# Second products of an attention and feed-forward kernel as 64-row pairs between key tiles, three visits per batch instead of seven

## The chip, the cores and the metric

The kernel runs on one core of one Trainium2 chip. The metric is device time in microseconds (us) of one execution; before the change it is 431.01, the median of three runs (430.65 to 431.02). Five engines work side by side: TensorE (PE, its weight loads shown as PEld), VectorE (DVE), ScalarE (ACT), GpSimd (POOL) and SyncE (SP). They meet through semaphores. PE writes its results into PSUM, which has eight banks here; DVE and ACT read them out.

## The reference

```
batch, n_heads, seq, head_dim = (8, 12, 448, 64)      # q, k, v: float32
q_n = q / (norm(q) + 1e-06);  k_n = k / (norm(k) + 1e-06)
scores = q_n @ k_n.T / tau                             # tau = 0.1
attn = exp(scores - max);  attn = attn / (sum(attn) + 1e-09)
x = (attn @ v), heads side by side                     # 3584 tokens x 768
h = x @ w_in                                           # 768 -> 2048
out = max(0.01 * h, h) @ w_out                         # 2048 -> 768
```

## The kernel before

**The work.** A *pair* is two heads of one batch (`s`, 48 of them, six per batch). Its q and k are loaded, squared and summed along the head (`squares` on POOL, `sums` on DVE), turned into norms (`roots`, an Ln and an Exp on ACT), divided by them (`normalise` on DVE) and transposed (`transposes`, from pair 12 on by a DMA of SP's queue). `hold` is a one-column copy on POOL that waits for the end of `normalise` ahead of the next `squares`. `roots` is two ACT instructions, so it stands in ACT's order between other activations.

**Key tiles.** A pair has three key tiles of 128 keys; the remaining 64 keys of two pairs share a fourth (`ki == 3`). `key_tiles` (L244) multiplies each key tile into two banks: two products, one per head, each on 64 rows of the array, since a head has 64 dimensions. The shared tile takes four products on quarters of the array. ACT then takes the exponential of both banks at once (L268).

**Attention of two pairs.** `attend(j)` (L527) sums the exponentials of four heads (`totals`, 16 products on 32-column strips into one bank, then an Ln and an Exp on ACT, L290 and L291), multiplies them with v (`products`, 32 strips into two banks), and `scale` writes the result to `xT` (DVE, L310).

**Feed-forward.** A *chunk* `c` is 384 columns of tokens (even `c`) or 512 (odd `c`), which become complete when batch `c` is attended. `first(c, m)` (L324) makes one of 16 slices of the hidden layer: six products of 128 rows into one bank and a Prelu on ACT (L340). `second(c, ts, half)` (L359) makes half of the output columns of 128 tokens: 16 products of 128 rows by 384 columns into one bank (L363), and a copy on DVE (L374). After the second half the rows are stored by SP's queue.

**The order of the work.** The order on each engine is that in which the program issues it. In the loop over batches (L599) the first and second groups of the chunk before stand in `queue`. From batch 2 on a batch has seven visits (`whole`, L582). Each issues, where it has one, the attention of two pairs (three of the seven do), then three key tiles, then the normalisation of one later pair (`sums`, `roots`, `normalise`, `transposes`, loads, `hold`, `squares` of the pair behind it, L612 to L631), then as many groups of `queue` as a share worked out from their costs allows (L604, L634). One group of the queue stays for the next batch. Behind the loop the last attention is followed by the group that is left and by the whole chunk 7.

**Banks.** `banks` (L77) deals the eight banks while the program is built: the one, or the aligned two, that was dealt longest ago, with those left out that are kept under a name until `given_back`. Whoever writes a bank waits for whoever read it last.

Of the kernel before, what the change touches and what calls it, by code (L numbers as in the profile page):

```python
# [8 lines left out]
F32 = mybir.dt.float32  # L9
# [7 lines left out]
def kernel(  # L17
# [10 lines left out]
    nc = tc.nc  # L28
    B, H, S, D = q.shape
    N_tok, D_model = out.shape  # L30
# [6 lines left out]
    NPAIR = H // 2  # L37
    NSLOT = B * NPAIR
    NQ = NPAIR // 2
    KT = D_model // 128  # L40
    MT = D_ff // 128
    HALF = D_model // 2
# [2 lines left out]
    ATTEND = 5500  # L45
    BLOCK = 1800
    SOON = 2
    assert REM == 64 and D == 64

    ctx.enter_context(tc.manual_schedule())  # L50
# [26 lines left out]
    def banks(count, keep=None, which=None):  # L77
        lo, hi = (0, 8) if not deals["apart"] else (0, 4) if count == 2 else (4, 8)
        x = which if which is not None else min(
            (i for i in range(lo, hi, count) if not set(range(i, i + count)) & set(kept.values())),  # L80
            key=lambda i: max(age[i : i + count]),
        )
        deals["n"] += 1
        age[x : x + count] = [deals["n"]] * count
        if keep:
            kept[keep] = x
        return ps[:, x] if count == 1 else ps[:, x : x + count]

    def given_back(keep):
        deals["n"] += 1  # L90
        age[kept.pop(keep)] = deals["n"]

# [26 lines left out]
    def load_qk(s, engs=(nc.sync, nc.sync)):  # L119
        if s >= NSLOT:  # L120
            return
        b, h0 = s // NPAIR, 2 * (s % NPAIR)
        q_h = ldp.tile([128, 2, 4, D], F32, name="q_h")
        k_h = ldp.tile([128, 2, 3, D], F32, name="k_h")
        engs[0].dma_start(out=q_h[:, :, 0:3], in_=main(q, b, h0, 2))
        engs[1].dma_start(out=k_h, in_=main(k, b, h0, 2))
        for i, (x, eng) in enumerate(zip((q, k), engs)):
            eng.dma_start(  # L128
                out=q_h[64 * i : 64 * i + 64, :, 3],
                in_=x[b, h0 : h0 + 2, MAIN:S].rearrange("h p d -> p h d"),  # L130
            )
        raw[s] = (q_h, k_h)
# [35 lines left out]
    def sums(s, parts=(0, 1)):  # L168
        if s >= NSLOT:
            return  # L170
        if s not in ss:
            ss[s] = smp.tile([128, 14], F32, name="ss")
        for i in parts:
            o = ss[s][:, 0:8] if i == 0 else ss[s][:, 8:14]
            nc.vector.tensor_reduce(  # L175
                o.rearrange("p (h t) -> p h t", h=2), sqs[s][i], axis=AX.X, op=ALU.add
            )

    def roots(s):
        if s >= NSLOT:  # L180
            return
        nc.scalar.activation(ss[s], ss[s], func=AF.Ln, bias=tiny)
        nc.scalar.activation(ss[s], ss[s], func=AF.Exp, scale=0.5)  # L183
        if s < 2:
            nc.scalar.activation(ss[s], ss[s], func=AF.Identity, bias=eps)
# [3 lines left out]
    def normalise(s):  # L189
        if s >= NSLOT:  # L190
            return
        r = smp.tile([128, 14], F32, name="r")
        if s >= 2:
            nc.vector.tensor_scalar_add(ss[s], ss[s], 1e-6)  # L194
        nc.vector.reciprocal(r, ss[s])  # L195
        qn[s] = qnp.tile([128, 7, 2, D], BF16, name="qn")
        for x, lo, hi, r0 in ((raw[s][0], 0, 4, 0), (raw[s][1], 4, 7, 8)):
            nt = hi - lo
            nc.vector.tensor_tensor(  # L199
                qn[s][:, lo:hi],  # L200
                x.rearrange("p h t d -> p t h d"),
                r[:, r0 : r0 + 2 * nt].rearrange("p (h t) -> p t h", h=2)
                .unsqueeze(3).to_broadcast([128, nt, 2, D]),
                op=ALU.mult,
            )
# [19 lines left out]
    def transposes(s):  # L225
        if s >= NSLOT:
            return
        dst = qtp.tile([128, 7, 128], BF16, name="qkT")
        qkT[s] = dst.rearrange("p t c -> p (t c)")
        if s >= DMA_FROM:  # L230
            nc.sync.dma_start(
                out=dst, in_=qn[s].rearrange("p t h d -> p (t h d)"), transpose=True
            )
            return
        tp = transposed()
        one(tp, s, 0, 7)
        nc.vector.tensor_copy(out=dst, in_=tp)  # L237
# [81 lines left out]
    def chunk_cols(c):  # L319
        return (0, MAIN) if c % 2 == 0 else (MAIN, 512)  # L320
# [27 lines left out]
    def rows_of(c, x, end):  # L348

        bb, rest = divmod(x, S)  # L350
        r0 = (2 * (c // 2) + bb) * S
        if rest >= MAIN:
            cnt = min(S - rest, end - x)
            return out[r0 + rest : r0 + rest + cnt], cnt
        t, p0 = divmod(rest, 128)
        cnt = min(128 - p0, end - x)
        return out[r0 : r0 + MAIN].rearrange("(p t) n -> t p n", t=3)[t, p0 : p0 + cnt], cnt

    def second(c, ts, half):  # L359
        c0, n = chunk_cols(c)  # L360
        po2 = banks(1)
        for m in range(MT):
            nc.tensor.matmul(  # L363
                out=po2[:, :HALF],
                lhsT=hT[c][:, m, ts * 128 : (ts + 1) * 128],
                rhs=w_out_sb[:, m, half * HALF : (half + 1) * HALF],
                start=(m == 0), stop=(m == MT - 1),
            )
        if half == 0:
            osb[c, ts] = osp.tile([128, D_model], F32, name="osb")  # L370
        o = osb[c, ts]
        last = c == B - 1 and ts == n // 128 - 1
        cut = HALF // 2 if last and half == 1 else HALF
        nc.vector.tensor_copy(out=o[:, half * HALF : half * HALF + cut], in_=po2[:, :cut])  # L374
        if cut < HALF:
            nc.scalar.copy(out=o[:, half * HALF + cut : (half + 1) * HALF], in_=po2[:, cut:HALF])
        if half == 1 or last:
            h0 = half * HALF if last else 0
            x, end, row = c0 + ts * 128, c0 + (ts + 1) * 128, 0
            while x < end:  # L380
                dst, cnt = rows_of(c, x, end)
                eng = nc.scalar if cut < HALF and row else nc.sync
                eng.dma_start(
                    out=dst[:, h0 : (half + 1) * HALF],
                    in_=o[row : row + cnt, h0 : (half + 1) * HALF],
                )
                x += cnt
                row += cnt


    work = {}
# [49 lines left out]
    def hold(x):  # L441
        seen = smp.tile([128, 1], F32, name="seen")
        gp.tensor_copy(out=seen, in_=x)  # L443
# [83 lines left out]
    def attend(j):  # L527
        totals(j)
        po = banks(2)
        for e in range(2):  # L530
            products(j, e, po[:, e])
        for e in range(2):
            scale(j, e)
# [63 lines left out]
    ]  # L597
    queue = []
    for b in range(1, B):  # L599
        queue += work[b - 1]  # L600
        units = opened if b == 1 else whole
        costs = [BLOCK + (ATTEND if at is not None else 0) for at, _, _ in units[1:] + [(2, 0, 0)]]
        for i, (at, tiles, ahead) in enumerate(units):
            share = (sum(g[0] for g in queue[:-1]) + sum(costs[i:])) / (len(units) - i) - costs[i]  # L604
            if b > 1 and i == 0:
                at = -1
            if at is not None:
                attend(b * NQ + at)
                load_v(b * NQ + at + 2)
            key_tiles([(b * NPAIR + p, ki) for p, ki in tiles])  # L610
            done = 0
            s = b * NPAIR + ahead if ahead else NSLOT  # L612
            if s < NSLOT:
                sums(s)
                roots(s)
            if b == 1 and i < 2:

                if i == 1:
                    cost, fn = queue.pop(0)
                    fn()  # L620
                    done += cost
                transposes(NPAIR + 4 + i)
            if s < NSLOT:
                normalise(s)
                if s >= DMA_FROM:
                    transposes(s)

                for n in (s + 2,) if s <= NPAIR + 6 else (s + 2, s + 3) if s == NPAIR + 7 else (s + 3,):
                    load_qk(n)
                hold(qn[s][:, 6, 0, 0:1])  # L630
                squares(s + 1)  # L631
            if at == 1:
                load_v_rem(b + 1)
            while len(queue) > 1 and (i == len(units) - 1 or done + queue[0][0] / 2 <= share):  # L634
                cost, fn = queue.pop(0)
                fn()
                done += cost
    attend(B * NQ - 1)
    for cost, fn in queue + work[B - 1]:
        fn()  # L640


# [33 lines left out]
```

## Time and profile before

| what | value |
|---|---|
| median of three runs | 431.01 us |
| the profiled execution's own time | 430.29 us |
| its span, first to last instruction | 428.4 us |
| PE busy, products | 414.7 us, 3315 of them |
| ACT busy | 255.4 us |
| DVE busy | 195.9 us |
| POOL busy | 137.3 us |
| second products, L363 | 896, 326 ns each from start to end |
| first products, L333 | 326 ns with 384 columns, 379 ns with 512 |
| strips, L279 | 352 to 356 ns each, four at once |
| exponential of a key tile, L268 | 144, 917 ns each |

A page of the profile describes one execution. Busy time of an engine is a union: products that run at the same time count once, and products overlap, each beginning before the one ahead has ended. So the length of one product is not its price; the price is read from how far apart products begin. The chain that ended last goes back from the last instruction, at each step to what released it or to the instruction before it on its engine. The timeline lists the instructions of all engines by their start; what stands in brackets is the idle time of the engine ahead of one and what ended it. Two batches together last 98.7 us there (batches 2 and 3 from 81.17 to 179.86, batches 4 and 5 from there to 278.54), so the middle of the kernel repeats every two batches.

### The profile page before, as it was taken

How to read it: one execution, taken by the hardware profiler on the slowest of the kernel's cores; microseconds unless marked ns; L12 is line 12 of the kernel's file. 1: busy time of each engine (PE TensorE's matmuls, PEld its weight loads, DVE VectorE, ACT ScalarE, POOL GpSimd, SP SyncE). 2: the span in 40 equal slices, each digit the busy share in tenths (PEclk: the TensorE clock that was granted, in tenths of full speed). 3: DMA queues.
4: the chain of work that ended last, by engine and by line, in shares of the span. 5: the costliest groups of instructions: out<-in, count | busy, mean ns of one | idle time of the engine just before them, and what ended most of it. 6: DMA issues, size and time to landing. Idle time of an engine off the chain costs nothing.

```text
span 428.4 us, 8636 instructions
## 1 busy us (share of the span) xinstructions
PE 414.7 (97%) x3315; PEld 208.2 (49%) x3329; DVE 195.9 (46%) x412; ACT 255.4 (60%) x448; POOL 137.3 (32%) x208
## 2 busy tenths in 40 slices
PE   7689999999999999999999999999999999999995
PEld 3234455544455555544455555544455555554563
DVE  5885867643453545354353554553444541220021
ACT  3987785667644785567553786658635586434300
POOL 4767533534124243513324132621424110000000
PEclk9999999999999999999999999999999999999999
DMA  7999997994558455953658456864448422110022
GB/s 174 187 240 229 211 217 135 186 207 104 108 121 166 103 125 95 224 108 84 127 101 160 104 127 129 168 113 136 91 103 161 100 61 42 39 73 2 0 75 74
DMA packets 102889, 53.66 MB, mean 125 GB/s; under 512 B 68928, under 2 KB 97856, under 8 KB 102848
## 3 DMA queue, kind: packets, MB, share of 16 engines
q1 hardware_dynamic: 77296, 40.98, 38.4%
q0 software_dynamic: 25056, 11.80, 22.0%
q8 instruction: 26, 0.43, 0.4%
q10 hardware_dynamic: 496, 0.33, 0.2%
q14 instruction: 15, 0.12, 0.1%
HBM read 45.61 MB, written 11.01 MB: 132 GB/s over the span
## 4 chain that ended last, share of the span: by engine, by line
PE 91%; DVE 3%; DMA 2%; issue 1%; SPq 1%; ACT 1%; POOL 0%; POOLq 0%; DVEq 0%
PE ps L363 35%; PE ps L333 34%; PE ps L279 13%; PE ps L256 9%; DVE qn L199 2%; DMA q_h<-in_q_dram 1%; PE ps L213 1%; DMA q_h<-in_k_dram 1%; SPq L128 1%; ACT pe L268 0%; DVE xT L310 0%; DVE ss L175 0%; DVE ss L194 0%; DVE r L195 0%; DVE qkT L237 0%
## 5 line engine op out<-in xcount | busy, mean ns | idle before, releaser
L268 ACT ACTIVATE pe<-ps 128x896 bf16<-128x896 f32 x144 | 122.5, 917 | 51.1 <-PE ps L256 50.0
L363 PE MATMUL ps<-w_out_sb,hT 128*128 128x384 bf16 x896 | 151.9, 326 | 0.0
L333 PE MATMUL ps<-xT,w_in_sb 128*128 128x384 bf16 (+1 forms) x757 | 150.6, 352 | 1.0 <-DVE xT L310 0.4
L363 PEld LDWEIGHTS <-hT 128*128 128x128 bf16 x896 | 85.2, 98 | 62.9 <-issue 8.4
L333 PEld LDWEIGHTS <-w_in_sb 128*128 128x128 bf16 x768 | 73.1, 98 | 72.9 <-issue 7.8
L340 ACT ACTIVATE hT<-ps 128x384 bf16<-128x384 f32 (+1 forms) x128 | 65.9, 541 | 46.7 <-PE ps L333 46.6
L374 DVE COPY osb<-ps 128x384 f32<-128x384 f32 (+1 forms) x56 | 30.9, 552 | 98.6 <-PE ps L363 92.1
L443 POOL CAST seen<-qn 128x1 f32<-128x1 bf16 x47 | 8.7, 184 | 207.7 <-DVE qn L199 201.9
L175 DVE TENSOR_REDUCE ss<-sq 128x8 f32<-128x512 f32 (+1 forms) x96 | 56.6, 614 | 19.2 <-POOL sq L164 16.9
L256 PE MATMUL ps<-qkT 64*128 64x448 bf16 (+1 forms) x384 | 46.1, 358 | 3.6 <-ACT pe L268 2.3
L164 POOL TENSOR_TENSOR sq<-q_h 128x512 f32<-128x512 f32 x46 | 47.8, 1038 | 3.7 <-DMA q_h<-in_k_dram 2.9
L310 DVE TENSOR_TENSOR xT<-ps,rb 128x448 bf16<-128x448 f32 x48 | 27.8, 619 | 32.5 <-ACT rb L291 32.5
L194 DVE TENSOR_SCALAR ss<-ss 128x14 f32<-128x14 f32 x46 | 9.2, 199 | 67.5 <-ACT ss L183 67.4
L164 POOL TENSOR_TENSOR sq<-k_h 128x384 f32<-128x384 f32 x46 | 37.8, 822 | 0.0
L290 ACT ACTIVATE rb<-ps 128x448 f32<-128x448 f32 x24 | 13.1, 544 | 38.9 <-PE ps L279 38.9
L279 PE MATMUL ps<-pe,v_b 128*32 128x448 bf16 x576 | 35.6, 353 | 0.0
L199 DVE TENSOR_TENSOR qn<-q_h,r 128x512 bf16<-128x512 f32 x48 | 33.5, 698 | 1.6
L256 PEld LDWEIGHTS <-qkT 64*128 64x128 bf16 (+1 forms) x384 | 13.0, 96 | 37.9 <-issue 31.5
L199 DVE TENSOR_TENSOR qn<-k_h,r 128x384 bf16<-128x384 f32 x48 | 26.5, 551 | 0.0
L268 ACT ACTIVATE pr<-ps 128x896 bf16<-128x896 f32 x24 | 22.2, 925 | 0.2 <-PE ps L256 0.2
L279 PEld LDWEIGHTS <-v_b 128*32 128x32 bf16 x576 | 15.2, 97 | 11.9 <-issue 0.4
L151 POOL DMA_DIRECT2D v_rem<-in_v_dram x32 | 20.4, 645 | 0.1
(40 smaller groups left out, 177.8 us busy)
## 6 DMA issues: line engine op xcount, KB each, us to landing
q_h<-in_q_dram SPq DMA_DIRECT2D x48, 192.0 KB, 3.1
k_h<-in_k_dram SPq DMA_DIRECT2D x47, 192.0 KB, 3.1
out_dram<-osb SPq DMA_DIRECT2D x30, 192.0 KB, 3.5
v_b<-in_v_dram POOLq DMA_DIRECT2D x24, 192.0 KB, 5.1
out_dram<-osb SPq DMA_DIRECT2D x12, 384.0 KB, 3.3
w_in_sb<-in_moe_w_in_dram POOLq DMA_DIRECT2D x4, 768.0 KB, 10.1
w_out_sb<-in_moe_w_out_dram POOLq DMA_DIRECT2D x2, 1536.0 KB, 18.5
q_h<-in_q_dram SPq DMA_DIRECT2D x48, 32.0 KB, 3.5
```

The source lines that it names most:

```text
L151: gp.dma_start(out=vrb[b % 2][lo : lo + 64, :, g], in_=r[g])
L164: eng.tensor_tensor(sq, x, x, op=ALU.mult)
L175: nc.vector.tensor_reduce(o.rearrange("p (h t) -> p h t", h=2), sqs[s][i], axis=AX.X, op=ALU.add)
L199: nc.vector.tensor_tensor(qn[s][:, lo:hi], x.rearrange("p h t d -> p t h d"), r[:, r0 : r0 + 2 * nt].rearrange("p (h t) -> p t h", h=2) .u ...
L256: nc.tensor.matmul(out=out[:, a, :S], lhsT=x[rows, c0:c1], rhs=x[rows, 0:S], start=True, stop=True,)
L268: nc.scalar.activation(out=dst, in_=sc[:, :, :S], func=AF.Exp, scale=inv_tau)
L279: nc.tensor.matmul(out=x[32 * g : 32 * g + 32, :S], lhsT=weights(g, ki) if ki < 3 else rem(g), rhs=pe[s][:, ki, a, :] if ki < 3 else pr[j] ...
L310: nc.vector.tensor_tensor(xT[m][:, 2 * jj + e, half * S : (half + 1) * S], pos.pop((j, e))[:, :S], rbs[j], op=ALU.mult,)
L333: nc.tensor.matmul(out=pm[:, :n], lhsT=w_in_sb[:, kt, m * 128 : (m + 1) * 128], rhs=xT[c // 2][:, kt, c0 : c0 + n], start=(kt == 0), stop= ...
L340: nc.scalar.activation(out=hT[c][:, m, :n], in_=pms.pop((c, m))[:, :n], func=AF.Prelu, alpha=0.01)
L363: nc.tensor.matmul(out=po2[:, :HALF], lhsT=hT[c][:, m, ts * 128 : (ts + 1) * 128], rhs=w_out_sb[:, m, half * HALF : (half + 1) * HALF], st ...
L374: nc.vector.tensor_copy(out=o[:, half * HALF : half * HALF + cut], in_=po2[:, :cut])
```

## The change

Up to batch 2 the loop stays, but batch 2 leaves six groups of the queue instead of one: three of the four token tiles of chunk 1. It also normalises one pair more in its last visit. From batch 3 on a batch has three visits. Each attends two pairs, then issues seven key tiles in three lots of two, three and two. Between the first and the second lot, and between the second and the third, stands one part of a token tile's second products, made by `both_halves`. Behind the key tiles come two normalisations and five or six first groups, the second normalisation in the middle of them. The token tiles are those of the chunk before the last, so they trail a chunk behind. A chunk with four of them puts its last one, by `second`, among the first groups of the first two visits.

`both_halves` takes the 128 rows of each hidden slice as two times 64 rows, which are multiplied at the same time into two banks. Part 0 adds up the upper rows for one half of the output columns and the lower rows for the other; part 1 does the crossed combinations into the same banks, then DVE copies both and the rows are stored. Ahead of the first products of part 1 stand two empty PE instructions that wait for the last products of part 0 in the same bank. The two banks are kept from part 0 to the copies. Behind the loop stand the last attention, six second groups of chunk 6 and the whole chunk 7.

```diff
+    APART = 6
+    MT_APART = 1
...
+    def both_halves(c, ts):
+        state = {}
+        def part(n):
+            if n == 0:
+                state["po"] = banks(2, ("rows", c, ts))
+            po2 = state["po"]
+            last = {}
+            for m in range(MT):
+                for h in range(2):
+                    rows, half = slice(64 * h, 64 * h + 64), h ^ n
+                    if n == 1 and m == 0:
+                        tc.add_manual_dep(
+                            nc.tensor.nop().ins,
+                            state["last"][half].ins.name,
...
+                        )
+                    last[half] = nc.tensor.matmul(
+                        out=po2[:, half, :HALF],
+                        lhsT=hT[c][rows, m, ts * 128 : (ts + 1) * 128],
+                        rhs=w_out_sb[rows, m, half * HALF : (half + 1) * HALF],
+                        start=(n == 0 and m == 0), stop=(n == 1 and m == MT - 1),
+                    )
+            state["last"] = last
+            if n == 1:
+                o = osp.tile([128, D_model], F32, name="osb")
+                for half in range(2):
+                    nc.vector.tensor_copy(
+                        out=o[:, half * HALF : (half + 1) * HALF], in_=po2[:, half, :HALF]
+                    )
+                given_back(("rows", c, ts))
+                store(o, c, chunk_cols(c)[0] + ts * 128, 0, D_model)
+        return lambda: part(0), lambda: part(1)
...
+    def norm(s):
+        if s >= NSLOT:
+            return
+        sums(s)
+        roots(s)
+        normalise(s)
+        transposes(s)
+        load_next(s)
+        hold(qn[s][:, 6, 0, 0:1])
+        squares(s + 1)
...
-    for b in range(1, B):
+    for b in range(1, 3):
         queue += work[b - 1]
+        keep = 1 if b == 1 else APART
...
+    visits = [
+        (-1, [(0, 0), (0, 1)], [(0, 2), (1, 0), (1, 1)], [(1, 2), (1, 3)]),
+        (0, [(2, 0), (2, 1)], [(2, 2), (3, 0), (3, 1)], [(3, 2), (3, 3)]),
+        (1, [(4, 0), (4, 1)], [(4, 2), (5, 0), (5, 1)], [(5, 2), (5, 3)]),
+    ]
+    tiles_left = [(1, ts) for ts in range(MT_APART, 4)]
+    for b in range(3, B):
+        firsts = [fn for _, fn in work[b - 1][:MT]]
+        more = []
+        if len(tiles_left) > len(visits):
+            c, ts = tiles_left.pop()
+            more = [lambda half=half: second(c, ts, half) for half in range(2)]
+        for i, (at, *parts) in enumerate(visits):
+            j, rows = b * NQ + at, both_halves(*tiles_left.pop(0))
+            attend(j)
+            load_v(j + 2)
+            if at == 1:
+                load_v_rem(b + 1)
+            for n, part in enumerate(parts):
+                key_tiles([(b * NPAIR + p, ki) for p, ki in part])
+                if n < 2:
+                    rows[n]()
+            fill_in = [firsts.pop(0) for _ in range(len(firsts) // (len(visits) - i))]
+            if more:
+                fill_in.insert(2, more.pop(0))
+            norm(b * NPAIR + 2 * i + 4)
+            for n, fn in enumerate(fill_in):
+                if n == len(fill_in) // 2:
+                    norm(b * NPAIR + 2 * i + 5)
+                fn()
+        tiles_left = [(b - 1, ts) for ts in range(chunk_cols(b - 1)[1] // 128)]
     attend(B * NQ - 1)
-    for cost, fn in queue + work[B - 1]:
+    for c, ts in tiles_left:
+        for half in range(2):
+            second(c, ts, half)
+    for _, fn in work[B - 1]:
         fn()
```

`kept` now holds lists of banks, so that two can be kept under one name; `store` is the storing part of `second`, and `load_next` the loads of a unit, both cut out unchanged.

More of the change, by code (lines that the diff above doesn't have):

```diff
@@ L79, in banks @@
         x = which if which is not None else min(
-            (i for i in range(lo, hi, count) if not set(range(i, i + count)) & set(kept.values())),
+            (i for i in range(lo, hi, count) if not set(range(i, i + count)) & set(sum(kept.values(), []))),
             key=lambda i: max(age[i : i + count]),
@@ L85, in banks @@
         if keep:
-            kept[keep] = x
+            kept[keep] = list(range(x, x + count))
         return ps[:, x] if count == 1 else ps[:, x : x + count]
@@ L90, in given_back @@
         deals["n"] += 1
-        age[kept.pop(keep)] = deals["n"]
+        for i in kept.pop(keep):
+            age[i] = deals["n"]
     w_in_sb = cpool.tile([128, KT, D_ff], BF16, name="w_in_sb")
@@ L377, in second @@
         if half == 1 or last:
[L378 to L388, printed above, removed]
+            store(o, c, c0 + ts * 128, half * HALF if last else 0, (half + 1) * HALF, cut < HALF)
@@ new lines, in store @@
+    def store(o, c, x, lo, hi, apart=False):
+        end, row = x + 128, 0
+        while x < end:
+            dst, cnt = rows_of(c, x, end)
+            eng = nc.scalar if apart and row else nc.sync
+            eng.dma_start(out=dst[:, lo:hi], in_=o[row : row + cnt, lo:hi])
+            x += cnt
+            row += cnt
+    def both_halves(c, ts):
[12 more added lines that the diff above has]
+                            state["last"][half].ins.name,
+                            mybir.DependencyInfo(
+                                mybir.DependencyClass.Sync, mybir.DependencyReason.DATA
+                            ),
+                            reason="the other rows' products in this bank",
+                        )
[15 more added lines that the diff above has]
+        return lambda: part(0), lambda: part(1)
@@ L597, with load_next @@
     ]
+    def load_next(s):
+        for n in (s + 2,) if s <= NPAIR + 6 else (s + 2, s + 3) if s == NPAIR + 7 else (s + 3,):
+            load_qk(n)
+    def norm(s):
[8 more added lines that the diff above has]
+        squares(s + 1)
     queue = []
-    for b in range(1, B):
+    for b in range(1, 3):
         queue += work[b - 1]
+        keep = 1 if b == 1 else APART
         units = opened if b == 1 else whole
@@ L603 @@
         for i, (at, tiles, ahead) in enumerate(units):
-            share = (sum(g[0] for g in queue[:-1]) + sum(costs[i:])) / (len(units) - i) - costs[i]
+            share = (sum(g[0] for g in queue[:-keep]) + sum(costs[i:])) / (len(units) - i) - costs[i]
             if b > 1 and i == 0:
@@ L611 @@
             done = 0
-            s = b * NPAIR + ahead if ahead else NSLOT
+            s = b * NPAIR + ahead if ahead else 3 * NPAIR + 3 if b == 2 else NSLOT
             if s < NSLOT:
@@ L626 @@
                     transposes(s)
-                for n in (s + 2,) if s <= NPAIR + 6 else (s + 2, s + 3) if s == NPAIR + 7 else (s + 3,):
-                    load_qk(n)
+                load_next(s)
                 hold(qn[s][:, 6, 0, 0:1])
@@ L633 @@
                 load_v_rem(b + 1)
-            while len(queue) > 1 and (i == len(units) - 1 or done + queue[0][0] / 2 <= share):
+            while len(queue) > keep and (i == len(units) - 1 or done + queue[0][0] / 2 <= share):
                 cost, fn = queue.pop(0)
```

## The prediction

> **What bounds the kernel now.** I read the page's busy times, its chain that ended last, that chain in order of time, and one stretch of the timeline of all engines. From the page:
>
> ```profile
> PE 414.7 (97%) x3315; PEld 208.2 (49%) x3329; DVE 195.9 (46%) x412; ACT 255.4 (60%) x448; POOL 137.3 (32%) x208
> PEclk9999999999999999999999999999999999999999
> PE 91%; DVE 3%; DMA 2%; issue 1%; SPq 1%; ACT 1%; POOL 0%; POOLq 0%; DVEq 0%
> ```
>
> TensorE (PE) is busy 97% at the full granted clock and is 91% of the chain; from batch 1 on the chain is PE alone. A saving must shorten PE's own sequence; a loss comes from anything that makes PE wait. The chain in order of time (start, length, piece), batch 3 into batch 4:
>
> ```profile
> 167.99 2.38 PE ps L279 x48
> 170.37 0.67 PE ps L256 x6
> 171.05 5.31 PE ps L363 x32
> 176.35 0.80 PE ps L256 x8
> 177.15 2.71 PE ps L363 x16
> ...
> 197.56 5.29 PE ps L333 x24
> ...
> 211.19 2.60 PE ps L363 x16
> ```
>
> Unit prices come from here. Sixteen second products follow other full-array products in 2.60, 0.1625 each, and follow key tiles in 2.71: **0.11 to come back to the full array** (32 in 5.31 says the same). First products of 512 columns: (5.29 - 0.11) / 24 = 0.216. On the line between 384 and 512 columns, 448 columns cost 0.189. A quad of strips (L279) costs (2.38 - 0.11) / 12 = 0.189, and a key tile, two 64-row products at once, the same: 0.67 = 3 x 0.189 + **0.10 to enter the 64-row shape**. The eight products of 0.80 hold one remainder tile in quarter arrays: 0.13 more for that shape.
>
> **Part 1, seven visits become three.** Now each batch has four visits without attention (full array to key tiles and back) and three with it. The key tiles of a changed visit lie in one 64-row stretch, between the strips before and the first products behind. So four entries and four returns fall away per batch, 4 x (0.10 + 0.11) = 0.85; the entries from strips, the three returns and the three remainder shapes stay. Five batches: **-4.24 us.**
>
> **Part 2, second products as 64-row pairs.** A token tile has 2 x 16 products of 0.1625 now, 5.2 us. Changed, it has two parts of 16 pairs. What a pair costs when 16 follow each other, adding up in two banks, no row shows. Nearest is the key tile, whose pair costs what one product of its columns costs, so I take 0.1625 and no change. A gain is excluded, since as many columns stream. The upper end: each pair also waits for its weights, 0.095 by the row of key-tile loads (92 to 103 ns), 480 pairs, +45.6. Against it stands this row of weight loads in one visit:
>
> ```profile
> 236.67 0.30 PEld L256 LDWEIGHTS <-qkT 64*128 64x128 bf16 x6 [0.37 <-issue]
> ```
>
> Six loads are 0.30 of busy time inside 0.67 in which PE streams three pairs: two lie beside each other, and later pairs' loads lie under running products of the same rows. The Trainium skill (TensorE: Matmul & The Clock Gate, Part 3, "The mechanism") says that a load overlaps running products only when its row group differs. By that rule the sum would be +45.6 higher; the row speaks against it.
>
> **Part 3, the explicit wait.** Part 1 of a tile begins with two empty PE instructions that wait for PE's own products of part 0. Queued behind are 16 pairs, and behind these the copies. Three key tiles (0.57) lie between, and a product's end is seen 0.36 after its start (the L374 copies). So I take 0. No row shows PE waiting for PE; the upper end is 0.36 in each of 15 tiles, +5.4.
>
> **Part 4, two normalisations close together: a new stall.** Now a unit has one, 6 us apart. Changed, the second `norm` of a visit stands two or three first groups (six products and a Prelu each) behind the first. `roots` of it sits on ScalarE (ACT) ahead of the Prelus (L340) of the remaining first groups. It waits for `sums`, these for the squares on POOL, these for `hold`, that for the first normalise. The links:
>
> ```profile
> 143.18 0.18 POOL L443 CAST seen<-qn 128x1 f32<-128x1 bf16 x1 [9.15 <-DVE qn L199]
> 143.39 1.03 POOL L164 TENSOR_TENSOR sq<-q_h 128x512 f32<-128x512 f32 x1
> ...
> 144.40 0.82 POOL L164 TENSOR_TENSOR sq<-k_h 128x384 f32<-128x384 f32 x1
> ...
> 144.46 1.35 DVE L175 TENSOR_REDUCE ss<-sq 128x8 f32<-128x512 f32 x2 [0.94 <-POOL sq L164]
> ...
> 147.18 0.33 ACT L182 ACTIVATE ss<-ss,tiny 128x14 f32<-128x14 f32 x1
> 147.54 0.21 ACT L183 ACTIVATE ss<-ss 128x14 f32<-128x14 f32 x1
> 147.66 1.24 ACT L340 ACTIVATE hT<-ps 128x384 bf16<-128x384 f32 x3
> ...
> 149.56 0.18 POOL L443 CAST seen<-qn 128x1 f32<-128x1 bf16 x1 [4.35 <-DVE qn L199]
> ...
> 155.74 0.54 ACT L290 ACTIVATE rb<-ps 128x448 f32<-128x448 f32 x1 [0.22 <-PE ps L279]
> ...
> 164.52 0.56 DVE L374 COPY osb<-ps 128x384 f32<-128x384 f32 x1 [2.33 <-PE ps L363]
> 165.00 1.14 DVE L175 TENSOR_REDUCE ss<-sq 128x8 f32<-128x512 f32 x2
> ```
>
> Count from R, the end of the second part's products on PE. Copies start at 0.20, 0.48 apart, then sums: end 0.20 + 0.96 + 1.14 = 2.30. Roots start 2.33 (the last exps, from 0.41 on and 0.8 apart, end at 2.14). Roots to hold: 149.56 - 147.18 = 2.38, so hold at 4.71. Hold to end of sums: 145.81 - 143.18 = 2.63, so 7.34. Second roots 7.37; Prelus 0.48 behind, 7.85, then 0.375 apart; Ln of the next totals 0.40 behind the third, 9.00 to 9.54.
>
> PE meanwhile: key tiles behind R 0.60, five first groups of 384 columns 30 x 0.1625 = 4.88, strips 2.38 with their entry 0.10, so the next visit's key tiles start at 7.96, its second at 8.16, the second products at 8.35. I dealt the eight banks by hand with the rule in `banks`: in this visit the second key tile takes the banks of the third and fourth first group (free at 8.71), and the second products take that of the fifth and that of the totals, free at 9.54. **PE waits 1.2 us.** The scales of the attended pair end near 11.3, before their bank is wanted at 12.1.
>
> The other visits: six first groups of 384 columns put PE at 9.32, wait 0.2. Five of 512 put it at 9.95 against 9.86 (longer Prelus): 0, with 0.1 to spare. Six of 512, or one more second group (+2.6): none. Batch 7 normalises only in its first visit, which has such a group. So 1.2 twice (batch 3), 0.2 twice (ends of batches 3 and 5): **+2.8 us.**
>
> **Part 5, the rest.** Batch 2 loses five second groups (13 us of PE work, done later at the same price). Its two visits with two first groups then have 3.4 us on PE against 4.1 on ACT (three exps 2.5, roots 0.57, two Prelus 1.07). Neighbours with 5.9 to 8.2 on PE take this up; followed visit by visit, each bank is free when PE comes: 0. If that cover were gone it would cost some 0.7 in each of the two, +1.4. The six second groups behind the last attention are work moved. Each `norm` still issues one transpose and four loads on SP (1.26 + 2.3 us); the next transpose comes 5 us later, so SP keeps up. The tile's stores stand ahead of them and wait for copies done by 1.24. POOL has the squares, then `load_v` (0.8) and the remainders (2.6), done before the next hold. Nothing of this is on the path.
>
> **Sum.** -4.24 + 2.8 = -1.5. The profiled execution took 430.29 (span 428.4 and 1.9 around it): 428.8. It is 0.7 below the median of the runs, 431.01; on that median the forecast is **429.5**. I call within 0.2% (0.86 us) the same, about what a measurement of this kernel can tell.
>
> **Rivals.**
> - *The banks are free in time* (some links overlap more than counted, or roots start earlier). For: 1.2 less in the count is enough. Then -4.24 to -2.5; at its end **426.8**. Chance 0.20.
> - *The normalisation chain is longer, slower than before.* Place: second roots on ACT, in the visits that have them. If the chain is e longer, four visits gain e of stall and, past 0.1, the four with 512-column products too: -1.5 + 4e + 4(e - 0.1). It passes +0.86 from **e = 0.34**; at e = 0.6 it is +2.9, **433.9**. For: seven handovers between engines, and in the batches of before ACT never waits for DVE's sums, so that link is not seen. Against: the links are measured in long pieces. Chance 0.22.
> - *The explicit waits empty PE's queue.* At 0.1 to 0.3 per tile 15 tiles cost 1.5 to 4.5: about the same to **432.5**. Against: 0.57 of key tiles stand ahead. Chance 0.10.
> - *The pairs' loads are not hidden*: 480 x 0.095 = 45.6 more, **475**. Chance 0.02, by the row of loads above. It is what that rule of the Trainium skill would do here.
> - *The stretch does not stay in one shape*, so the change doesn't do what it says: no saving, the stall stays, +2.8: **433.8**. Against: key tiles pass into one another without a gap. Chance 0.04.
> - The forecast, -2.5 to -0.4 (428.5 to 430.6): chance 0.42.
>
> Faster: 0.37 of the forecast and the first rival, 0.57. Same: 0.05 of the forecast, 0.05 of the third, 0.04 of the second: 0.14. Slower: 0.29. The range 426.5 to 433.0 leaves out the far half of the second rival and the last large ones, some 0.18.
>
> **What would show it.** Right: four entries to 64-row work per batch gone; row pairs every 0.1625; PE waiting for ACT (L290, L340) in batch 3 about 1.2 per visit and hardly elsewhere; second roots 7.4 after R. Wrong: pairs above 0.167 apart (each 0.005 is 2.4 us), gaps ahead of the second part, waits of PE in batches 4 and 6, or in batch 2.

## The result and the profile after

| | before | changed | ratio to before, 95% interval |
|---|---|---|---|
| median, same chip | 430.67 us | 428.83 us | 0.9957 [0.9942, 0.9971] |
| again, in a second series | 430.71 us | 429.33 us | 0.9974 [0.9962, 0.9986] |
| profiled execution (span) | 430.29 (428.4) | 428.73 (426.8) | |

The change makes the kernel 1.4 to 1.8 us faster; the forecast was 1.5. Both intervals leave out 1, but the second reaches to 0.9986, inside the 0.2% that the prediction calls the same. Of the page of the changed kernel, the lines that answer to those of before:

```profile
PE 413.7 (97%) x3809; PEld 214.0 (50%) x3809; DVE 197.0 (46%) x412; ACT 255.5 (60%) x448; POOL 137.0 (32%) x208
PE 87%; DVE 5%; ACT 2%; DMA 2%; POOL 1%; SPq 1%; issue 1%; POOLq 0%; DVEq 0%
```

PE has 480 products more, since 960 of 64 rows (L415) stand where 480 of 128 rows stood; its busy time has not grown, since they run two at a time. (The counts of the two pages differ by 494, since some records are missing from the trace of before.) PE has lost 4% of the chain to DVE, ACT and POOL, which before had no part of it from 44.3 us up to the last copies. The chain in order of time shows what a changed visit is where nothing is late (batch 4):

```profile
184.22 2.38 PE ps L282 x48
186.60 0.49 PE ps L259 x4
187.09 2.60 PE ps L415 x32
189.69 0.57 PE ps L259 x6
190.26 2.60 PE ps L415 x32
192.86 0.50 PE ps L259 x6
193.36 6.58 PE ps L336 x30
```

L282 are the strips, L259 the key tiles, L415 the pairs, L336 the first products. Sixteen pairs take 2.60, as 16 products of the full array did, and three key tiles between them 0.57, without the 0.10 of an entry. By the records of two batches in the middle (179 to 277), PE went from the full array to 64 rows and back eight times before, four a batch, and not once in the changed kernel; the entries from the strips and those by the quarters are as many as before. The visit shown is 15.72 long, all of it PE's own work. And here is the visit behind which PE has to wait (batch 3):

```profile
131.35 1.02 DVE osb L425 x2
132.38 1.06 DVE ss L178 x2
...
133.46 0.32 ACT ss L185
...
136.04 1.83 POOL sq L167 x2
...
138.48 0.32 ACT ss L185
...
139.03 1.14 ACT hT L343 x3
140.17 0.45 ACT rb L293
...
140.66 2.76 PE ps L415 x31
```

It is the chain of part 4 of the prediction, link for link: copies, sums, roots, normalise and hold (left out here), squares, sums (left out), second roots, Prelus, Ln of the totals, and only then the second products.

### The profile page after: what moved, and what is told of

It reads as the page before. It is cut to its first block, busy times and chain, and to the rows that moved or that the text cites. A ratio compares the mean times of both kernels' runs of the same rounds, so it can differ in the third digit from the quotient of the medians.

```text
span 426.8 us, 9601 instructions
## 1 busy us (share of the span) xinstructions
PE 413.7 (97%) x3809; PEld 214.0 (50%) x3809; DVE 197.0 (46%) x412; ACT 255.5 (60%) x448; POOL 137.0 (32%) x208
## 4 chain that ended last, share of the span: by engine, by line
PE 87%; DVE 5%; ACT 2%; DMA 2%; POOL 1%; SPq 1%; issue 1%; POOLq 0%; DVEq 0%
PE ps L336 32%; PE ps L415 18%; PE ps L366 16%; PE ps L282 12%; PE ps L259 8%; DVE qn L202 2%; POOL sq L167 1%; DVE ss L178 1%; DMA q_h<-in_q_dram 1%; PE ps L216 1%; DMA q_h<-in_k_dram 1%; ACT hT L343 1%; SPq L131 1%; DVE osb L425 0%; ACT pe L271 0%
## 5 line engine op out<-in xcount | busy, mean ns | idle before, releaser
L336 PE MATMUL ps<-xT,w_in_sb 128*128 128x384 bf16 (+1 forms) x768 | 151.6, 353 | 0.5 <-DVE xT L313 0.5
L336 PEld LDWEIGHTS <-w_in_sb 128*128 128x128 bf16 x768 | 73.0, 98 | 71.5 <-issue 6.7
L343 ACT ACTIVATE hT<-ps 128x384 bf16<-128x384 f32 (+1 forms) x128 | 64.3, 538 | 41.8 <-PE ps L336 41.2
L415 PE MATMUL ps<-w_out_sb,hT 64*128 64x384 bf16 x960 | 83.9, 323 | 0.3
L366 PE MATMUL ps<-w_out_sb,hT 128*128 128x384 bf16 x416 | 70.0, 326 | 0.0
L415 PEld LDWEIGHTS <-hT 64*128 64x128 bf16 x960 | 49.0, 94 | 32.7 <-issue 2.4
L366 PEld LDWEIGHTS <-hT 128*128 128x128 bf16 x416 | 40.1, 98 | 28.2 <-issue 2.1
L259 PE MATMUL ps<-qkT 64*128 64x448 bf16 (+1 forms) x384 | 49.2, 357 | 3.7 <-ACT pe L271 2.3
L425 DVE COPY osb<-ps 128x384 f32<-128x384 f32 x30 | 15.3, 553 | 72.2 <-PE ps L415 72.2
L185 ACT ACTIVATE ss<-ss,tiny 128x14 f32<-128x14 f32 x48 | 14.9, 311 | 49.1 <-DVE ss L178 49.0
L377 DVE COPY osb<-ps 128x384 f32<-128x384 f32 (+1 forms) x26 | 14.3, 549 | 58.2 <-PE ps L366 58.2
L282 PE MATMUL ps<-pe,v_b 128*32 128x448 bf16 x576 | 35.6, 353 | 0.0
L259 PEld LDWEIGHTS <-qkT 64*128 64x128 bf16 (+1 forms) x384 | 15.4, 96 | 33.5 <-issue 24.9
```

Source lines behind the costliest of these rows:

```text
L259: nc.tensor.matmul(out=out[:, a, :S], lhsT=x[rows, c0:c1], rhs=x[rows, 0:S], start=True, stop=True,)
L282: nc.tensor.matmul(out=x[32 * g : 32 * g + 32, :S], lhsT=weights(g, ki) if ki < 3 else rem(g), rhs=pe[s][:, ki, a, :] if ki < 3 else pr[j] ...
L336: nc.tensor.matmul(out=pm[:, :n], lhsT=w_in_sb[:, kt, m * 128 : (m + 1) * 128], rhs=xT[c // 2][:, kt, c0 : c0 + n], start=(kt == 0), stop= ...
L343: nc.scalar.activation(out=hT[c][:, m, :n], in_=pms.pop((c, m))[:, :n], func=AF.Prelu, alpha=0.01)
L366: nc.tensor.matmul(out=po2[:, :HALF], lhsT=hT[c][:, m, ts * 128 : (ts + 1) * 128], rhs=w_out_sb[:, m, half * HALF : (half + 1) * HALF], st ...
L415: last[half] = nc.tensor.matmul(out=po2[:, half, :HALF], lhsT=hT[c][rows, m, ts * 128 : (ts + 1) * 128], rhs=w_out_sb[rows, m, half * HALF ...
```

## The experiments

How much a version gains is read best as the time from the first of the strips that open batch 2 to the start of the last product on PE, since those strips begin anywhere from 80.72 to 81.61 in the profiles, whichever version runs. It is 342.40 before and 340.85 in the changed kernel. The theory: **no shape is entered needlessly (-4.24), and ACT's order holds back banks in four visits (+2.7)**. The main rival: the banks are simply too few while a pair of them is kept, and the gain and the loss have other sizes.

**Second normalisation behind the first groups.**

```diff
             for n, fn in enumerate(fill_in):
-                if n == len(fill_in) // 2:
-                    norm(b * NPAIR + 2 * i + 5)
                 fn()
+            norm(b * NPAIR + 2 * i + 5)
```

> The second normalisation of a visit stands behind all its first groups instead of in their middle. Theory (late second roots on ACT hold back the Prelus and the next totals' Ln, and PE waits for their banks): the Prelus are done by 6.2 after R, second roots run from 7.4 to 7.9, Ln ends at 8.4 against 8.35 at which PE wants the bank; nearly all of the 2.6 us of stall (1.16 twice, 0.16 twice in the changed kernel) goes: 426.3. Rival (the stall comes from eight banks being too few while a pair is kept for the second products, whatever ACT's order): no gain, 428.8.

Measured: 426.11, ratio to before 0.9899 [0.9883, 0.9916]; 338.17 from batch 2 on, 2.68 less than the changed kernel. ACT in the visit that stalled (start, length):

```profile
137.14 0.49 ACT L343 ACTIVATE hT<-ps 128x384 bf16<-128x384 f32 x1 [0.48 <-PE ps L336]
138.77 0.31 ACT L185 ACTIVATE ss<-ss,tiny 128x14 f32<-128x14 f32 x1 [1.15 <-DVE ss L178]
139.12 0.21 ACT L186 ACTIVATE ss<-ss 128x14 f32<-128x14 f32 x1
139.24 0.53 ACT L293 ACTIVATE rb<-ps 128x448 f32<-128x448 f32 x1
```

The last Prelu no longer stands behind the roots; it follows its own products. The Ln ends at 139.77, 8.3 after R (the end of the second part's products on PE, 131.45 here). The banks are the same eight, the same pair is kept: the rival falls.

**First normalisation ahead of part 0.**

```diff
                 key_tiles([(b * NPAIR + p, ki) for p, ki in part])
+                if n == 0:
+                    norm(b * NPAIR + 2 * i + 4)
                 if n < 2:
                     rows[n]()
...
-            norm(b * NPAIR + 2 * i + 4)
-            for n, fn in enumerate(fill_in):
-                if n == len(fill_in) // 2:
-                    norm(b * NPAIR + 2 * i + 5)
+            norm(b * NPAIR + 2 * i + 5)
+            for fn in fill_in:
                 fn()
```

> The first normalisation of a visit stands between the first lot of key tiles and part 0, the second ahead of the first groups. Theory: the chain begins some 6 us earlier, second roots follow the last exps at 2.3 after R, no bank is late: all 2.6 us go, 426.2, and PE waits nowhere from batch 2 on. Rival (too few banks): 428.8. A loss would mean that the moved roots hold back the exps of the second lot.

Measured: 426.29, ratio 0.9903 [0.9888, 0.9918]; 338.16 from batch 2 on. The same place of the chain, now PE alone:

```profile
136.54 2.38 PE ps L282 x48
138.93 0.48 PE ps L259 x4
139.41 2.60 PE ps L415 x32
```

The second roots start 2.3 after R here. Two different orders, in neither of which the second roots hold back a Prelu, end within 0.01 us of each other, 4.23 and 4.24 below before. That is the saving of the shapes by itself, counted as 4.24.

**Both again, beside the changed kernel, on one chip.**

> The changed kernel once more, beside the two versions that follow, so that they are compared on one chip. 1.5 to 2.0 below the kernel before, as in the first result.

> The version with the second normalisation behind all first groups, again: 2.4 below the changed kernel (its PE ended 2.4 earlier in the first look). Rival, that the difference between chips made it: less than 1.

> The version with the first normalisation ahead of part 0, again: 2.6 below the changed kernel and within 0.6 of the version before it, since neither has a wait of PE left to remove.

Measured: 429.33, 426.23 and 426.44, or 0.9974 [0.9962, 0.9986], 0.9901 [0.9888, 0.9915] and 0.9906 [0.9890, 0.9922] of before. So 3.1 and 2.9 below the changed kernel where 2.4 and 2.6 were expected. From batch 2 on the three are 340.82, 338.17 and 338.16: the excess over 2.66 is not in that stretch. In the profiled executions as a whole the two are 2.7 and 2.4 below, so the excess is put down to the scatter of the runs, which is not shown further. These two versions beat both kernels, by 1.0% of before; they are the same within what is measured.

**The parts on the full array.** `h` and the explicit wait go; the rest of the visit stays.

```diff
-                for h in range(2):
-                    rows, half = slice(64 * h, 64 * h + 64), h ^ n
...
-                    last[half] = nc.tensor.matmul(
-                        out=po2[:, half, :HALF],
-                        lhsT=hT[c][rows, m, ts * 128 : (ts + 1) * 128],
-                        rhs=w_out_sb[rows, m, half * HALF : (half + 1) * HALF],
-                        start=(n == 0 and m == 0), stop=(n == 1 and m == MT - 1),
-                    )
+                nc.tensor.matmul(
+                    out=po2[:, n, :HALF],
+                    lhsT=hT[c][:, m, ts * 128 : (ts + 1) * 128],
+                    rhs=w_out_sb[:, m, n * HALF : (n + 1) * HALF],
+                    start=(m == 0), stop=(m == MT - 1),
+                )
```

> The two parts stay where they are and keep the same two banks, but each is 16 products of 128 rows for one half of the columns, without the explicit wait. Theory (the saving is the changes of shape): four changes more in each of 15 visits, 2 x 0.21 each, +6.4; PE comes later to the late banks and part 0 needs only the earlier of the two, which takes 1.6 off the stall: 433.6. Rival (pairs are as dear as what they save, and the gain came from elsewhere, fewer visits or other waits): within 1 us of 428.8.

Measured: 433.38, ratio 1.0068 [1.0053, 1.0083]; 345.12 from batch 2 on, 4.27 more than the changed kernel. Three visits with second products of the old shape are *slower* than the seven of before. A visit of batch 4 in its chain (L404 are the products of the parts):

```profile
202.93 0.48 PE ps L259 x4
203.42 2.71 PE ps L404 x16
206.12 0.67 PE ps L259 x6
206.80 2.71 PE ps L404 x16
209.50 0.61 PE ps L259 x6
```

Against the changed visit of batch 4 each part has 0.11 more and the key tiles behind each 0.10 and 0.11: 0.43 per visit, 6.4 in 15. The rest is stall. It is 0.3 in each of two visits of batch 3 instead of 2.7 in all, where I expected 0.5: 6.4 - 2.7 + 0.6 = 4.3, as measured. Per batch this version goes from the full array to 64 rows and back six times, the kernel before four times: two more in each of five batches are 2 x 0.21 x 5 = 2.1, and with 0.6 of stall 2.7, as measured against before (345.12 - 342.40). So the pairs, not the fewer visits, are the gain.

**A longer chain.**

```diff
         hold(qn[s][:, 6, 0, 0:1])
+        if s + 1 < NSLOT:
+            idle = sqp.tile([128, 2, 4, D], F32, name="idle")
+            gp.tensor_tensor(idle, raw[s + 1][0], raw[s + 1][0], op=ALU.mult)
         squares(s + 1)
```

> One more square of q on POOL (1.04 us, its result unused) ahead of the squares in every normalisation of batches 3 to 7, so the chain to the second roots is e = 1.04 longer. Theory: +1.04 in the four visits that stall and +0.95 in the four with five first groups of 512 columns, nothing in those with six or with a second group among them: +7.9, 436.7. Rival (too few banks, or the stall does not hang on the roots): 428.8 to 429.3.

Measured: 436.87, ratio 1.0149 [1.0131, 1.0168]; 349.78 from batch 2 on, 8.93 more. The second roots come 8.26 after R, not 7.33, so e is 0.93, and by the formula of the second rival 4e + 4(e - 0.1) = 7.0. The other 1.9 needs a second cause, so that the time came out within 0.2 of the 436.7 is in part luck. Most of it is one stretch of the profile. Busy time of each engine in the stretch with the stall and in the one behind it (start and end, length, busy us with instructions, PEclk, DMA share, GB/s):

```profile
138.70:142.10 3.40, 2.29 (x23) 0.91 (x17) 2.18 (x6) 2.83 (x8) 0.53 (x2) 1.00 0.37 108
142.10:145.50 3.40, 3.40 (x25) 1.88 (x23) 1.02 (x2) 1.45 (x2) 3.18 (x4) 0.50 0.73 169
```

Behind a wait of 2.1 us the granted clock is halved for 3.4 us, and eleven of the 16 pairs there start 0.32 apart instead of 0.16: 3.4 / 2 = 1.7. With 7.0 that is 8.7 of 8.93. So the sensitivity of the chain was counted rightly, and a stall may have a second price that I had not counted. It is not paid every time: the next visit of this profile has a wait of the same 2.1 (from 156.8 on) with the clock at 1.00 behind it, the changed kernel's waits of 1.2 show no drop, and of this version's four runs one (436.42) had a mean clock of 1.000 where a spell of 3.4 us would leave 0.996. What decides it stays open; that the wait brings the drop about is seen once and not shown.

**The wait uncovered.**

```diff
                 key_tiles([(b * NPAIR + p, ki) for p, ki in part])
-                if n < 2:
-                    rows[n]()
+                if n == 0:
+                    rows[0]()
+                    rows[1]()
```

> Both parts directly behind each other after the first lot, the other five key tiles of the visit behind them, so that nothing covers the explicit wait. Theory: a product's end is seen 0.36 after its start, so the first pair of part 1 starts 0.36 to 0.5 behind the last of part 0 instead of 0.16, in each of 15 tiles: 3 to 5 us in all from the waits. Rival (the wait costs nothing in any place, because PE's own order satisfies it): 0.16. The time as a whole grows more than by the waits, some 10 to 40, since five key tiles in a row find too few free banks and the normalisations come later; it is not what is read here.

Measured in a single execution: 450.99. The two parts in its chain:

```profile
125.16 2.62 PE ps L415 x32
127.78 0.05 issue
127.82 2.77 PE ps L415 x32
```

The first pair of part 1 starts 0.38 to 0.39 behind the last of part 0 in all 15 tiles, instead of 0.16. So the wait costs 0.22 where nothing covers it, 3.3 in 15 tiles, and nothing in the changed kernel: there part 1 starts 0.19 behind the last key tile in every visit without a stall, which is a key tile's own price. No version without the wait was run, so whether PE's own order would do without it is not shown.

## Why the prediction was right, point by point

- **Part 1, -4.24.** Right. With the stall taken away the kernel is 4.23 to 4.24 below before from batch 2 on.
- **Part 2, no change by the pairs.** Right: 0.1625 a pair over 16 pairs, with sums kept in two banks. Their loads lie under running products of the same rows (32 products in 2.60 while each load lasts 0.094), as the single row of before already said. So what the Trainium skill (TensorE: Matmul & The Clock Gate, Part 3, "The mechanism") lists as found in traces, that a load overlaps running products only when its row group differs, does not hold here; the same section also lets a load into the background weight buffer go ahead, which would fit, but no run here shows which buffer is used.
- **Part 3, no cost of the explicit wait.** Right, with its uncovered price now known: 0.22, below my upper end of 0.36.
- **Part 4, the stall.** Right in mechanism, place and nearly in size. Count and measurement from R (131.15): second roots 7.37 and 7.33, end of Ln 9.54 and 9.47, start of the second products 9.5 and 9.51 against 8.35 wanted. Twice 1.16 and twice 0.18 make 2.68 where I had 2.8. Inside batches 4 and 6, within 0.1 of a stall by the count, there is none above 0.02.
- **Part 5, nothing from the rest.** Right from batch 2 on: in the two versions without the stall nothing is left over beside the 4.24.
- **Where to look was partly wrong.** I expected the stall among PE's waits for ACT. The list of PE's waits has no row for it. Four products that start late by 0.15 to 0.43 hide under the 0.35 that each counts as busy: PE shows 45.23 busy of 45.60 in batch 3 although it lost 2.3 there. The chain in order of time shows it, and so do the starts of the products.
- **The rival with the longer chain** has nearly the right formula (7.0 for e = 0.93, where 8.93 less the 1.7 of the clock is 7.2), but no price for a drop of the clock, which stood behind one of that run's two waits of 2.1.
- **Smaller errors of the prediction.** -4.24 + 2.8 is -1.4, not -1.5. The third rival's upper end, 15 x 0.3 = 4.5 on 429.5, is 434.0, not 432.5. Before the change the chain is PE alone from 44.3 us on; the strips and key tiles of batch 1 begin at 37.2, with some ACT and DVE between.

## What to carry to other kernels

Where PE is the whole chain, count how often its sequence changes the shape of the array, and see whether full-array work next to smaller products can be cut into that shape: it ran at the same rate and saved the change on both sides. Two steps of one chain that used to lie a visit apart must be followed through every engine's order when they move together; here a short activation that waited for the chain held back everything queued behind it, and the banks with it. More than half of a gain can be lost to such an order: here moving one call gave 2.7 us more, above the 1.55 that the change itself had kept of its 4.24.

## What the runs showed of the hardware

- **Price of a shape**, start to start, beyond the product itself: 0.10 from the full array to 64 rows (three key tiles in 0.67 instead of 0.57) and 0.11 back (16 products in 2.71 instead of 2.60); 0.09 from 64 rows to quarters (0.28 between starts instead of 0.19) and 0.13 from quarters to the full array (0.315 instead of 0.19).
- **The two halves of a pair are separate streams.** In the stall of the changed kernel the first product of one half started at 140.22 and of the other at 140.66. From there on one half ran 0.14 ahead, through 16 pairs, three key tiles and 16 pairs more, until the next change of shape. It cost nothing beyond the later half: the three key tiles took 0.57 and the 16 pairs behind them 2.61.
- **A half-clock spell of 3.4 us** appeared in the middle of the kernel once, behind a stretch of 3.4 us of which PE had waited 2.1 (an equal wait one visit later brought none), and in four profiles 14 to 18 us from the start. There it is not seen to cost anything: batch 2 begins at 80.85 to 81.50 with it and at 80.72 to 81.61 without. The Trainium skill (TensorE: Matmul & The Clock Gate, Part 1, the table of the two states) names at least one idle window of about 3.4 us as the condition; here PE shows 2.29 busy in the 3.4 us ahead of the spell.
